# The split weights in DRAM laid out in runs of 2048 bytes a partition, in a linear attention with a gated feed-forward

## The chip, the cores and the metric

One Trainium2 chip, one of its cores. The metric is the device time of one execution in microseconds (us), as the median of several runs. TensorE is called PE here, VectorE DVE, ScalarE ACT, GpSimd POOL and SyncE SP, as in the profile.

## What is computed

The reference is a linear attention followed by a gated feed-forward net, all in float32:

```python
q_s = softmax(q, over the head's 64 columns);  k_s = softmax(k, over the 576 positions)
kv = k_s.T @ v;  attn = q_s @ kv            # for each of 8 batches and 8 heads
x = attn as (4608, 512);   xn = x / sqrt(mean(x*x) + 1e-6) * rms_g
out = (silu(xn @ w_gate) * (xn @ w_val)) @ w_out                        # w_gate, w_val: 512 x 1536, w_out: 1536 x 512
```

## The kernel before

The 4608 tokens are cut into nine blocks of 512 columns. A product of float32 numbers is made of three products of a reduced float32 type: each operand is split into a high part (a rounded copy) and a low part (the remainder), and high times high, high times low and low times high are summed. So each weight exists as a pair of halves.

A hand-written list, `ORDER`, gives the steps in the order in which they are issued. Each step is one of the functions below, its numbers after the dots; the letter behind a colon names the engine. Every engine works through its own instructions in that order, and an instruction that waits holds up all that stand behind it on the same engine.

The work has three stages:

- Blocks 0 to 2 (to about 375 us) go one by one, while the attention of later blocks is made beside them. For a chunk `s` (12 chunks of 128 hidden columns to a block) the weights' halves are made by `w_hi` and `w_lo` in a tile named `w` (two buffers), and by `o_hi` and `o_lo` in a tile named `o` (two buffers). `f1` (L973) multiplies them with `x`, `f2` (L1010) with the hidden values `hh` and `hl` that `h_hi` and `h_lo` (L994) make. In block 1 the halves are also written to DRAM by SP: `w_keep` (L917, 12 of them) and `o_keep` (L921, 12). SP further writes sums and differences of the weights, split in the same way, with `s_keep` (L958, 24). In the last six chunks of block 2 (30 to 35) the halves aren't made again but reloaded: `w_back` (L925) and `o_back` (L929), six each.
- Blocks 3 to 8 go in three pairs. A pair's first products use one level of Strassen's scheme: `pp.p.i.m.k` (L1122) is product k of pair p, chunk pair i, matrix m (gate or value), six matmuls each. Its weights come from DRAM through four tiles called the ring, one for each matrix m and each part: part 1 holds four of the eight stored parts and part 2 three. `w_in.p.i.m.part` (L1095) reloads one such tile as soon as the last product that reads it is done; there are 72. Their destination stands in the trace as `ring` or `w`.
- The last products use `o` in pair 0 (`f2p`, L1215, with 24 reloads `o_in`, L1107) and a second Strassen level in pairs 1 and 2 (`qq`, L1331, whose weights SP loads in `qw`, L1276 and L1279, partly from the same DRAM tensors `od`).

All reloads of `w_back`, `o_back`, `w_in` and `o_in`, 108 in all, are issued on POOL's own DMA queue. POOL also does a share of the arithmetic: `q_sub` and `q_mul` for the attention (L730, L759), low parts such as `h_lo` (L994), `b_lo` (L1078) and `n_lo` (L821), and sums such as `t_add` (L1066). The program is built with `dynamic_dma_scratch_size=1024`, the room in each partition of SBUF that is set aside for the descriptors of POOL's DMAs.

The DRAM tensors are `wd` (six, one for two chunks) and `od` (twelve). Before the change a partition's eight parts of one matrix lie together in `wd`, 2048 bytes each: a part-1 reload reads one run of 8192 bytes from each of 128 partitions, a part-2 reload one of 6144, a `w_back` two of 4096; an `o_in` or `o_back` reads one run of 4096.

Of the kernel before, what the change touches and what calls it, by code (L numbers as in the profile page):

```python
# [8 lines left out]
F32 = mybir.dt.float32  # L9
I32 = mybir.dt.int32  # L10
U32 = mybir.dt.uint32
F32R = mybir.dt.float32r
# [334 lines left out]
def linear_attention_then_gated_ffn(ctx: ExitStack, tc, q, k, v, w_gate, w_val, w_out, rms_g, out):  # L347
    nc = tc.nc
    B, H, S, D = q.shape
    NT, DM = out.shape  # L350
    DF = w_gate.shape[1]
    P = 128
    NG = H // 2
    NKT = DM // P
    NF = DF // P
# [14 lines left out]
    NH = NF // 2  # L370
    HALF = TB // 2
    assert NB == JP + 2 * NPAIR and NKT == 4 and NF == 2 * NH

    wsp = ctx.enter_context(tc.tile_pool(name="wsp", bufs=2))
# [29 lines left out]
    def on(default):  # L404
        return unit[0] or default
# [467 lines left out]
    wh_, wo_, h_, po, g_, v_ = {}, {}, {}, {}, {}, {}  # L873
    ov = out.rearrange("(j t p) m -> j t p m", p=P, t=T)
    ov0 = out.rearrange("(j p t) m -> j t p m", p=P, t=T)

    def w_tile(s):
        if s not in wh_:
            wh_[s] = wsp.tile([P, 2, 2, 2, HALF], F32R, name="w")
        return wh_[s]  # L880

    def o_tile(s):
# [9 lines left out]
    def w_hi(s, a, n):  # L892
        copy(w_tile(s)[:, a:a + n, :, 0], halves(s % NF, a, n), nc.scalar)

    def w_lo(s, a):
        w = w_tile(s)[:, a]
        on(nc.gpsimd).tensor_tensor(out=w[:, :, 1], in0=halves(s % NF, a, 1)[:, 0], in1=w[:, :, 0].bitcast(F32),  # L897
                                    op=ALU.subtract)
# [6 lines left out]
        on(nc.vector).tensor_tensor(out=ol, in0=W(s % NF, 2), in1=oh.bitcast(F32), op=ALU.subtract)  # L905

    S2, S1, A11, A12, A21, A22, S3, S4 = range(8)
    wd = [tc.dram_tile([2, P, 8, 2, HALF], F32, name=f"wd{i}") for i in range(NH)]
    od = [tc.dram_tile([P, 2, DM], F32, name=f"od{i}") for i in range(NF)]
    ot_ = {}  # L910

    def parts_of(i, at, n):
        return wd[i][:, :, at:at + n].rearrange("m p a b f -> p m a (b f)")

    def w_keep(s):
        i, odd = divmod(s % NF, 2)
        on(nc.sync).dma_start(parts_of(i, A21 if odd else A11, 2),  # L917
                          wh_[s].rearrange("p m a b f -> p m a (b f)").bitcast(F32))

    def o_keep(s):  # L920
        on(nc.sync).dma_start(od[s % NF], ot_[s].bitcast(F32))  # L921

    def w_back(s):
        i, odd = divmod(s % NF, 2)
        nc.gpsimd.dma_start(w_tile(s).rearrange("p m a b f -> p m a (b f)"), parts_of(i, A21 if odd else A11, 2))  # L925

    def o_back(s):
        o = wsp.tile([P, 2, DM], F32R, name="o")
# [26 lines left out]
        on(nc.gpsimd).tensor_tensor(out=t[:, :, 1], in0=f, in1=t[:, :, 0].bitcast(F32), op=ALU.subtract)  # L955

    def s_keep(i, n):
        on(nc.sync).dma_start(parts_of(i, {1: S1, 2: S2, 3: S3, 4: S4}[n], 1)[:, :, 0],  # L958
                          split[i, n].rearrange("p m b f -> p m (b f)").bitcast(F32))

    done = {}
# [57 lines left out]
    XF, XO, RING, WO, H2, TMP, HH = {}, {}, {}, [], {}, {}, {}  # L1019
# [61 lines left out]
    def ring():  # L1081
        if not RING:
            t0 = big.tile([P, 6, TB], F32R, name="ring_0", tag="raw_0")
            t1 = big.tile([P, 6, TB], F32R, name="ring_1", tag="raw_1")
            RING[1] = [t0[:, :4]]
            RING[2] = [t1[:, :3], t1[:, 3:]]
            WO.append(t0[:, 4:])

    def w_in(p, i, m, part):
        ring()  # L1090
        if part == 1 and m == len(RING[1]):
            RING[1].append(wsp.tile([P, 4, TB], F32R, name="w"))
        t = RING[part][m].rearrange("p a b -> p (a b)")
        src = wd[i][m, :, :4] if part == 1 else wd[i][m, :, 5:]
        nc.gpsimd.dma_start(t, src.rearrange("p a b f -> p (a b f)"))  # L1095

    def o_in(p, t, c):
        ring()
# [309 lines left out]
    def e_put(x, h):  # L1408
# [7 lines left out]
              n_t, n_y0, n_y1, o_hi, o_lo, q_c0, q_eps0, q_exp, q_half, q_half2, q_hi, q_lo, q_load, q_load0, q_max,  # L1416
              q_max0, q_max2, q_mul, q_mul0, q_rec, q_rec0, q_sub, q_sub0, q_sum, q_sum0, q_sum2, q_t, q_t0, q_x, q_x0,
              silu, store, w_keep, o_keep, w_back, o_back, s_add, s_hi, s_lo, s_keep, x_cp, x_nm, t_add, b_hi, b_lo,
              w_in, o_in, r_keep, r_load, t_sum, t_hi, t_lo, t_keep, qw, q_t1, q_t2, q_t3, q_t4, qb_hi, qb_lo, qq, qs1, qu2, qu3,
              q22, q21, q12, qtr, qput, qpua, pp, c_s1, c_u2, c_u3, c_11, c_21, c_22, c_12, gate, hm, e_add, e_tr, e_copy, e_put, hp_hi, hp_lo, f2p, put, v_load, v_ones, w_hi, w_lo, warm, x_acc, x_hi, x_lo, x_sq)}  # L1420

# [33 lines left out]
```

## Time and profile before

| | us |
|---|---|
| median of three runs | 941.9 (941.64, 941.9, 947.51) |
| the profiled execution, its own time | 938.76 |
| its span, first to last instruction | 937.0 |

The profiled execution's own time is 1.76 us above its span and 3.1 us under the median. Times in rows count from the start of the span. A timeline row gives start, duration, engine, line, operation, names (written <- read), and in brackets the idle time before it with what ended it.

### The profile page before, as it was taken

The numbers are of one execution on the slowest core, as the hardware profiler recorded it, in microseconds if no ns is written. First come the engines' busy times: TensorE is split into PE (matmuls) and PEld (weight loads), VectorE is DVE, ScalarE is ACT, GpSimd is POOL, SyncE is SP. The second block draws the span as 40 slices with busy tenths as digits, with TensorE's granted clock in tenths as the row PEclk, the third lists the DMA queues.
The fourth block names the chain that finished last, engine by engine and source line by source line (L and its number), as shares of the span: only waits on it lengthen the run. The fifth ranks groups of instructions, "written<-read, shape, count | busy, mean of one in ns | idle before, by whom it ended". The sixth has DMA issues, their size and how long they took to land.

```text
span 937.0 us, 14321 instructions
## 1 busy us (share of the span) xinstructions
PE 917.7 (98%) x4601; PEld 744.2 (79%) x4601; DVE 729.1 (78%) x1530; ACT 469.0 (50%) x749; POOL 535.2 (57%) x552
## 2 busy tenths in 40 slices
PE   7999999998999999999999999999999999999998
PEld 5578877886887888888888888878888888888886
DVE  7899879987979998877887788766469965645586
ACT  5898847765678766464553364222215522111241
POOL 5887879877677987667763635333432423332403
PEclk8999999999999999999999999999999999999999
DMA  9996628889977999898986799889665788855255
GB/s 244 301 261 195 159 45 283 283 277 304 304 249 211 225 254 260 231 269 222 237 217 203 228 272 285 275 270 298 204 199 175 212 194 278 267 189 179 71 155 91
DMA packets 214203, 212.65 MB, mean 227 GB/s; under 512 B 136816, under 2 KB 175472, under 8 KB 209520
## 3 DMA queue, kind: packets, MB, share of 16 engines
q1 hardware_dynamic: 191472, 122.86, 47.7%
q0 software_dynamic: 16320, 88.09, 30.3%
q10 hardware_dynamic: 6336, 0.79, 0.6%
q8 instruction: 37, 0.61, 0.3%
q14 instruction: 38, 0.31, 0.1%
HBM read 161.35 MB, written 50.33 MB: 226 GB/s over the span
## 4 chain that ended last, share of the span: by engine, by line
PE 88%; DMA 5%; SPq 2%; DVE 2%; issue 1%; ACT 1%; POOL 1%; DVEq 0%; ACTq 0%; POOLq 0%
PE ps_gv L973 18%; PE ps_gv L1122 18%; PE ps_o L1122 11%; PE ps_o L1010 9%; PE ps_a L1122 7%; PE ps_o L1331 6%; PE ps_o L1215 4%; PE ps_a L1331 3%; PE ps_gv L1331 3%; PE ps_a L577 2%; PE ps_a L1215 2%; PE ps_gv L1215 2%; PE ps_a L785 2%; DMA w<-in_moe_w_val_dram 1%; SPq L520 1%
## 5 line engine op out<-in xcount | busy, mean ns | idle before, releaser
L973 PE MATMUL ps_gv<-xh,w 128*128 128x512 f32 x576 | 190.1, 397 | 1.1 <-DVE gs L985 0.8
L1122 PE MATMUL ps_gv<-x,ring 128*128 128x512 f32 x576 | 143.0, 392 | 0.0
L973 PEld LDWEIGHTS ps_gv<-xh,w 128*128 128x128 f32 x576 | 108.2, 188 | 26.2 <-DVE gs L985 0.9
L1122 PEld LDWEIGHTS ps_gv<-x,ring 128*128 128x128 f32 x576 | 107.0, 188 | 23.0
L973 PE MATMUL ps_gv<-xl,w 128*128 128x512 f32 x288 | 111.6, 391 | 0.0
L1143 DVE TENSOR_TENSOR tmp<-tmp,ps_gv 128x512 f32<-128x512 f32 x84 | 57.3, 684 | 49.3 <-PE ps_gv L1122 47.5
L1122 PE MATMUL ps_o<-x,ring 128*128 128x512 f32 x360 | 85.4, 390 | 0.9 <-DVE tmp L1143 0.9
L1095 POOL DMA_DIRECT2D ring<-wd x54 | 31.0, 575 | 92.3 <-PE ps_o L1122 37.1
L1122 PEld LDWEIGHTS ps_o<-x,ring 128*128 128x128 f32 x360 | 67.5, 188 | 15.4 <-DVE tmp L1143 1.3
L1010 PE MATMUL ps_o<-o,hh 128*128 128x512 f32 x288 | 73.2, 396 | 0.0
L973 PEld LDWEIGHTS ps_gv<-xl,w 128*128 128x128 f32 x288 | 54.2, 188 | 10.6 <-issue 0.4
L1010 PEld LDWEIGHTS ps_o<-o,hh 128*128 128x128 f32 x288 | 53.0, 188 | 11.2 <-issue 0.4
L897 POOL TENSOR_TENSOR w<-w,w 128x512 fp32r<-128x512 f32 x36 | 48.8, 1366 | 4.6 <-ACT w L409 3.8
L1143 DVE TENSOR_TENSOR tmp<-tmp,ps_o 128x512 f32<-128x512 f32 x42 | 28.6, 684 | 27.4 <-PE ps_o L1122 24.3
L409 ACT CAST hh<-gs 128x512 fp32r<-128x512 f32 x48 | 29.5, 615 | 29.9 <-DVE gs L985 16.0
L1095 POOL DMA_DIRECT2D w<-wd x18 | 10.1, 559 | 58.0 <-PE ps_a L1122 37.8
L534 DVE TENSOR_REDUCE cm<-kt 128x128 f32<-128x640 f32 x28 | 36.7, 1310 | 4.4 <-DMA kt<-in_k_dram 4.4
L1010 PE MATMUL ps_o<-o,hl 128*128 128x512 f32 x144 | 38.7, 391 | 0.0
L1122 PE MATMUL ps_a<-x,w 128*128 128x512 f32 x144 | 36.9, 392 | 0.0
L1122 PE MATMUL ps_a<-x,ring 128*128 128x512 f32 x144 | 36.7, 390 | 0.0
L994 POOL TENSOR_TENSOR hl<-gs,hh 128x512 fp32r<-128x512 f32 x20 | 26.8, 1340 | 16.9 <-ACT hh L409 10.8
L1122 PE MATMUL ps_gv<-x,w 128*128 128x512 f32 x144 | 35.1, 391 | 0.0
(634 smaller groups left out, 2306.8 us busy)
## 6 DMA issues: line engine op xcount, KB each, us to landing
ring<-wd POOLq DMA_DIRECT2D x36, 768.0 KB, 5.7
w<-wd POOLq DMA_DIRECT2D x24, 1024.0 KB, 6.0
ring<-wd POOLq DMA_DIRECT2D x18, 1024.0 KB, 5.5
wd<-w SPq DMA_DIRECT2D x12, 1024.0 KB, 5.0
wd<-parts SPq DMA_DIRECT2D x24, 512.0 KB, 3.7
o<-od POOLq DMA_DIRECT2D x18, 512.0 KB, 5.9
od<-o SPq DMA_DIRECT2D x12, 512.0 KB, 3.9
out_dram<-ot SPq DMA_DIRECT2D x20, 256.0 KB, 4.3
```

The lines of the kernel that those rows point to most:

```text
L409: (e.copy if e is nc.scalar else e.tensor_copy)(dst, src)
L534: nc.vector.tensor_reduce(out=cm, in_=kt_[b, g].rearrange("p h j d -> p h d j"), axis=AX.X, op=ALU.max)
L577: nc.tensor.matmul(pk[h * D:(h + 1) * D, :D + 1], lhsT=ke[:n, h, j], rhs=vt[:n, j, h], start=(j == 0), stop=(j == len(rows) - 1))
L897: on(nc.gpsimd).tensor_tensor(out=w[:, :, 1], in0=halves(s % NF, a, 1)[:, 0], in1=w[:, :, 0].bitcast(F32), op=ALU.subtract)
L973: nc.tensor.matmul(pd[s], lhsT=w[:, a, c // 2, m, c % 2 * P:c % 2 * P + P], rhs=X[j, c][x], start=(n == 1), stop=(n == 3 * NKT))
L994: on(nc.gpsimd).tensor_tensor(out=hl, in0=g_[s], in1=h_[s][0].bitcast(F32), op=ALU.subtract)
L1010: nc.tensor.matmul(po[t], lhsT=a[:, t * P:(t + 1) * P], rhs=w, start=(i == 0 and n == 0), stop=(i == NF - 1 and n == len(terms) - 1))
L1095: nc.gpsimd.dma_start(t, src.rearrange("p a b f -> p (a b f)"))
L1122: nc.tensor.matmul(abc[p, i, m, b], lhsT=src[:, h, c * P:(c + 1) * P], rhs=operand(o, c, x), start=first and n == 0, stop=n == 5, skip_gro ...
L1143: nc.vector.tensor_tensor(out=dst, in0=ux[u + (src,)], in1=abc[u + (b,)], op=ALU.add)
L1215: nc.tensor.matmul(pa[p, t, k], lhsT=a[:, k * P:(k + 1) * P], rhs=w, start=(c == 0 and n == 0), stop=(c == NF - 1 and n == 2))
L1331: nc.tensor.matmul(qacc[p, b, x], lhsT=ws[l][x], rhs=h[m], start=first and i == 0 and n == 0, stop=i == NH - 1 and n == 2, skip_group_chec ...
```

## The change

The tile `w` and the DRAM tensors get another order of the same elements. In `wd` each of the eight parts of each matrix becomes a block of 128 partitions by 2048 bytes; `od` becomes two such blocks. Inside the tile `w` the two matrices' parts alternate. All transfers of these tensors by `w_keep`, `o_keep`, `s_keep`, `w_back`, `o_back` and `w_in`, `o_in` then consist of runs of 2048 bytes. `qw` still reads runs of 1024 bytes from `od`. No step is added, left out or moved, and no engine changes.

```diff
     def w_tile(s):
         if s not in wh_:
-            wh_[s] = wsp.tile([P, 2, 2, 2, HALF], F32R, name="w")
+            wt_[s] = wsp.tile([P, 4, 2 * HALF], F32R, name="w")
+            wh_[s] = wt_[s].rearrange("p (k m) (b f) -> p m k b f", k=2, b=2)
         return wh_[s]
...
-    wd = [tc.dram_tile([2, P, 8, 2, HALF], F32, name=f"wd{i}") for i in range(NH)]
-    od = [tc.dram_tile([P, 2, DM], F32, name=f"od{i}") for i in range(NF)]
+    wd = [tc.dram_tile([8, 2, P, 2 * HALF], F32, name=f"wd{i}") for i in range(NH)]
+    od = [tc.dram_tile([2, P, DM], F32, name=f"od{i}").rearrange("m p f -> p m f") for i in range(NF)]
     def parts_of(i, at, n):
-        return wd[i][:, :, at:at + n].rearrange("m p a b f -> p m a (b f)")
+        return wd[i][at:at + n].rearrange("k m p f -> p (k m) f")
     def w_keep(s):
         i, odd = divmod(s % NF, 2)
-        on(nc.sync).dma_start(parts_of(i, A21 if odd else A11, 2),
-                          wh_[s].rearrange("p m a b f -> p m a (b f)").bitcast(F32))
+        on(nc.sync).dma_start(parts_of(i, A21 if odd else A11, 2), wt_[s].bitcast(F32))
     def w_back(s):
         i, odd = divmod(s % NF, 2)
-        nc.gpsimd.dma_start(w_tile(s).rearrange("p m a b f -> p m a (b f)"), parts_of(i, A21 if odd else A11, 2))
+        w_tile(s)
+        nc.gpsimd.dma_start(wt_[s], parts_of(i, A21 if odd else A11, 2))
     def s_keep(i, n):
-        on(nc.sync).dma_start(parts_of(i, {1: S1, 2: S2, 3: S3, 4: S4}[n], 1)[:, :, 0],
+        on(nc.sync).dma_start(parts_of(i, {1: S1, 2: S2, 3: S3, 4: S4}[n], 1),
                           split[i, n].rearrange("p m b f -> p m (b f)").bitcast(F32))
     def w_in(p, i, m, part):
...
-        t = RING[part][m].rearrange("p a b -> p (a b)")
-        src = wd[i][m, :, :4] if part == 1 else wd[i][m, :, 5:]
-        nc.gpsimd.dma_start(t, src.rearrange("p a b f -> p (a b f)"))
+        src = wd[i][:4, m] if part == 1 else wd[i][5:, m]
+        nc.gpsimd.dma_start(RING[part][m], src.rearrange("k p f -> p k f"))
```

## Rows read from the trace of the kernel before

**Rows 1.** The page, part 1: busy time, share, instructions.
```profile
PE 917.7 (98%) x4601; PEld 744.2 (79%) x4601; DVE 729.1 (78%) x1530; ACT 469.0 (50%) x749; POOL 535.2 (57%) x552
```
**Rows 2.** Windows: length, busy by engine, granted clock, DMA share, GB/s.
```profile
310.00:370.00 60.00, 60.00 (x340) 49.10 (x339) 53.82 (x142) 39.93 (x63) 50.36 (x57) 1.00 1.07 265
412.00:937.00 525.00, 519.74 (x2414) 426.50 (x2412) 372.75 (x706) 178.12 (x300) 219.38 (x231) 1.00 0.74 216
```
**Rows 3.** PE's waits, 310 to 937 us: total, times, longest.
```profile
PE ps_o L1122 <- DVE tmp L1143: 0.9, 1, 0.9
```
**Rows 4.** DMA queues: packets, MB, share of 16 engines' span.
```profile
q0 software_dynamic: 16320, 88.09, 30.3%
...
q10 hardware_dynamic: 6336, 0.79, 0.6%
```
**Rows 5.** Groups of POOL's instructions by form: count, busy us, mean ns, idle before.
```profile
L1095 POOL DMA_DIRECT2D ring<-wd x54 | 31.0, 575 | 92.3 <-PE ps_o L1122 37.1 <-PE ps_a L1122 28.7 <-PE ps_gv L1122 23.1
...
L925 POOL DMA_DIRECT2D w<-wd x6 | 4.7, 784 | 4.6 <-PE ps_gv L973 4.3 <-issue 0.3
```
**Rows 6.** DMA issues: count, KB each, median us from issue to landing.
```profile
wd<-parts SPq DMA_DIRECT2D x24, 512.0 KB, 3.7
...
od<-o SPq DMA_DIRECT2D x12, 512.0 KB, 3.9
```
**Rows 7.** POOL's timeline, 305 to 332 us: first and last of six reloads.
```profile
310.46 0.89 POOL L925 DMA_DIRECT2D w<-wd  x1
...
328.02 0.75 POOL L925 DMA_DIRECT2D w<-wd  x1 [0.26 <-issue]
```
**Rows 8.** Timeline of ACT and PE, 333 to 338 us.
```profile
333.38 0.63 ACT L734 ACTIVATE qt<-qt 128x512 f32<-128x512 f32 x1 [1.87 <-POOL qt L730]
...
334.94 0.73 ACT L569 ACTIVATE kt<-kt 128x640 f32<-128x640 f32 x1
...
336.80 0.80 PE L577 MATMUL ps_a<-vt,kt 128*64 128x65 f32 x20
```
**Rows 9.** POOL's timeline, 356 to 362 us.
```profile
356.14 0.77 POOL L925 DMA_DIRECT2D w<-wd  x1 [2.40 <-PE ps_gv L973]
356.91 0.55 POOL L1095 DMA_DIRECT2D ring<-wd  x1
...
358.74 1.28 POOL L1066 TENSOR_TENSOR ot<-xl,xh 128x512 f32<-128x512 f32 x1
...
361.05 0.55 POOL L1107 DMA_DIRECT2D x<-od  x1
```
**Rows 10.** Timeline of ACT and PE, 358 to 364 us.
```profile
360.59 0.61 ACT L409 CAST hh<-gs 128x512 fp32r<-128x512 f32 x1
...
363.68 0.62 PE L1010 MATMUL ps_o<-o,hh 128*128 128x512 f32 x2
```
**Rows 11.** Landings of the reloads issued at 356.14 (L925) and 356.91 (L1095).
```profile
DMA to landing us min/median/max: 5.6/5.6/5.6
...
DMA to landing us min/median/max: 8.4/8.4/8.4
```
**Rows 12.** Timeline of POOL and PE, 408 to 411 us.
```profile
409.03 1.29 POOL L821 TENSOR_TENSOR ql<-acc,qh 128x512 fp32r<-128x512 f32 x1
...
410.38 0.49 PE L835 MATMUL ps_a<-ql,mean_w 128*128 128x512 f32 x1
```
**Rows 13.** The reload with the least to spare: issue, landing, first matmul.
```profile
559.96 0.57 POOL L1107 DMA_DIRECT2D o<-od  x1
...
DMA to landing us min/median/max: 7.6/7.6/7.6
...
568.84 0.61 PE L1215 MATMUL ps_a<-o,hh 128*128 128x512 f32 x2
```
**Rows 14.** Timeline of POOL and PE, 380 to 384 us.
```profile
381.34 1.29 POOL L994 TENSOR_TENSOR hl<-gs,hh 128x512 fp32r<-128x512 f32 x1
...
383.40 0.84 PE L1010 MATMUL ps_o<-o,hl 128*128 128x512 f32 x3
```

More of the change, by code (lines that the diff above doesn't have):

```diff
@@ L875, in linear_attention_then_gated_ffn @@
     ov0 = out.rearrange("(j p t) m -> j t p m", p=P, t=T)
+    wt_ = {}
     def w_tile(s):
         if s not in wh_:
-            wh_[s] = wsp.tile([P, 2, 2, 2, HALF], F32R, name="w")
+            wt_[s] = wsp.tile([P, 4, 2 * HALF], F32R, name="w")
+            wh_[s] = wt_[s].rearrange("p (k m) (b f) -> p m k b f", k=2, b=2)
         return wh_[s]
```

## The prediction

> **What bounds the kernel now.** I read the page's busy shares first: PE is busy 98% of the span, POOL 57%, ACT 50% [rows 1]. Then the windows: POOL's reloads run from 310 us on, and from there PE is busy 60.00 of 60 us, then 519.7 of 525, at a granted clock of 1.00, while the DMA share is 1.07 and then 0.74 [rows 2]. Then PE's waits after 310: one, of 0.9 us, for DVE, and none for a DMA [rows 3]. So PE's matmuls set the time and every reload lands in time. The change touches no matmul; it can only matter where something that it makes later reaches PE, and it can hardly win anything, since after 310 PE lost 0.9 us to waits and some 4 us at the very end.
>
> How much the reloads have to spare: the tightest of the 108 is an `o_in` issued at 559.96, landed 7.6 us later, used at 568.84, 1.3 us to spare [rows 13]. Followed in the same way, none of the other 107 has under 2.
>
> **Packets.** A `w_in` of part 1 goes from 128 runs to 512, one of part 2 from 128 to 384, a `w_back` from 256 to 512, an `o_in` or `o_back` from 128 to 256. Before: 72 x 128 + 6 x 256 + 30 x 128 = 14,592, and with 16 small ones for each of 108 DMAs 16,320, the count of the queue [rows 4]. After: 36 x 512 + 36 x 384 + 6 x 512 + 30 x 256 = 43,008, with the small ones 44,736.
>
> **What a packet costs the DMA.** On SP's queue 512 KB in packets of 2048 bytes (`s_keep`) land after 3.7 us and the same in packets of 4096 (`o_keep`) after 3.9 [rows 6]: nothing. From above: the 6336 packets of queue q10, of 125 bytes on average, take 0.6% of 16 engines' 937 us, 14 ns each [rows 4], so no more than that is fixed. 384 more packets over 16 engines are then at most 0.34 us for a reload. With the longer issue (next part) a reload lands 0.2 to 1.0 us later, under the spare of 1.3 of the tightest, which itself gains only 128 packets (0.1 + 0.2 us). Late data costs PE nothing; I take 0.
>
> **What a packet costs POOL.** An issue of 128 packets takes 575 ns, one of 256 (`w_back`, the only such form) 784 [rows 5]: 0.21 us for 128 more. A `w_in` becomes 0.63 (part 1) or 0.42 us longer, a `w_back` 0.42, an `o_in` or `o_back` 0.21; in all 36 x 0.63 + 36 x 0.42 + 6 x 0.42 + 30 x 0.21 = 46.6 us of POOL, which is busy for 50.4 + 219.4 of the 585 us of the two windows [rows 2] and so has room. From below, the 0.21 us may be the price of the third dimension of the access pattern, not of packets: then every `w_in` and `o_in` costs 0.21 and `w_back` nothing. From above, the issue grows in proportion to the packets, 2.3 us for 512 (a rival below). I take 0.21 for 128. The Trainium skill's page DMA: Bandwidth & Descriptors (section Anatomy of one DMA) says that one can emit a lot of descriptors before the incremental cost shows up; by it terms A and B below would be 0, but the row of 784 against 575 speaks against it.
>
> Where does a longer POOL reach PE? Where POOL's next instruction is used at once.
> A. Between 310.46 and 328.02 six reloads are issued [rows 7]: three `w_back`, two o-reloads, a `w_in` of part 2, 3 x 0.42 + 2 x 0.21 + 0.42 = 2.1 us more. Behind them POOL's `q_sub` releases ACT at 333.38; behind that on ACT `k_exp` ends at 335.67, and PE's `k_mm` starts at 336.80 [rows 8]: 1.13 to spare. So PE is 0 to 1.0 late, by how much of the 2.1 POOL's short idle times there take up; I take 0.5.
> B. Right behind a `w_in` at 408.43 POOL makes `n_lo`, which ends at 410.32, and PE's `n_sum` takes it at 410.38 [rows 12]: 0.06 to spare, so PE is 0.6 late.
> At other places I found spare. A + B = 1.1 us.
>
> C. **Room for descriptors.** POOL writes the descriptors of its DMAs into a scratch of 1,024 bytes a partition. Before, the largest pile is at 361.05: five reloads issued in 4.9 us [rows 9], none landed (the first does at 356.14 + 5.6 = 361.74, [rows 11]): 256 + 4 x 128 = 768 packets under way, and no issue waits. After, the same five make 512 + 512 + 384 + 256 + 256 = 1,920, and the first two alone 1,024, beside 256 of an `o_back` that hasn't quite landed. Whether that fits, no row shows: the cost is between 0 and a wait of POOL for the landing of what came before. I take the wait, since the pile is 2.5 times what the trace shows to fit.
> The Trainium skill's page DMA: Bandwidth & Descriptors (sections Terms and The descriptor swizzle) gives 16 bytes to a descriptor and 9 on each engine, the completing one included, to 1 MiB in 128 partitions. By it the scratch holds 64 an engine; the five reloads before take 53, which agrees with rows 9, and two of 512 packets take 66; the wait would fall where I put it.
> The price, from rows: the `w_in` at 356.91 stands until `w_back.35` has landed, 361.74 + 0.42 = 362.2, then takes 1.2 instead of 0.55 us, so POOL goes on at 363.4 instead of 357.46, 5.9 late. Behind it stand two `t_add` (L1066, to 360.02), for which ACT waits with the `hh` of `f2.33` behind it, ready at 361.20; PE takes that at 363.68 [rows 9, 10], 2.5 to spare: PE 3.4 late. Next the `o_back` stands until that `w_in` has landed, 5.6 to 8.4 us [rows 11] after 362.2, 367.8 to 370.6; POOL gets there at 363.4 + 2.55 + 0.97 = 366.9, so 0.9 to 3.7 more. Behind it are low parts for the first `pp` and the `hl` of `f2.34`, which has 383.40 - 382.63 = 0.8 to spare [rows 14]. Some of it falls into POOL's idle times; I take 1 of 0 to 3.7. Later an `o_in` now and then follows a `w_in` closely; such places may add up to the same 3.7 once more, I take 0. In the pairs a reload is issued every 5 to 6 us (96 of them in 525 us [rows 2]) and the one before it is about to land (512 + 384 under way), so nothing stands. C = 4.4, bounds 0 and 10.8.
>
> SP's side: 12 `w_keep` and 12 `o_keep` of block 1 double their packets. Their landing shows no price [rows 6]; if each took 0.3 us longer, ACT and DVE, which reuse the tiles, would be late by that at a few places: 0, bound 1. `w_hi` and `w_lo` write the same runs of 256 elements at other places of the tile: 0, covered by ACT's 50% [rows 1].
>
> Sum: 1.1 + 4.4 = +5.5 us against the profiled execution's 938.76, 944.3. The median of the runs shown lies 3.1 above that execution, so I give 941.9 + 5.5 = 947.4.
>
> **The rivals.**
> No wait for room: the scratch holds it, or frees places while a transfer runs. For it: no row shows POOL waiting for its own queue. Then only A + B: 943.0.
> SP's transfers gain, since they meet 2048-byte packets on the same engines instead of 8192, or the change does nothing. For it: a DMA share of 1.07 in 310 to 370 [rows 2]. Against: PE waits for no DMA there, so no more than the 0.9 us of [rows 3] comes back: 941.0 to 941.9.
> POOL becomes the bound between 310 and 370 (slower): the issue grows with the packets, 0.575 us for 128 more. In that window stand six `w_back`, seven o-reloads, two `w_in` of part 2 and one of part 1: 6 x 0.78 + 7 x 0.57 + 2 x 1.15 + 1.73 = 12.7 us more on 50.4 busy of 60 [rows 2]: 3.1 too much, with B at 1.7 and C at its 3.4 + 3.7 = 7.1: +11.9, 953.8. It decides from where POOL's idle 9.6 us are used up, 9.6 / 12.7 x 0.575 = 0.43 us for 128 packets, twice the price of [rows 5]. Against it: 256 packets cost 784 ns, not 1150.
>
> **How the numbers follow.** The wait for room, 947.4: 0.50. No wait, 943.0: 0.30. SP gains or nothing happens, 941 to 942: 0.06. POOL as the bound, 953.8: 0.14. One per cent is 9.4 us, about what a measurement of this kernel can tell from no change. Slower by more: most of the last case, 0.11, and a fifth of the first, whose bounds reach +11.9, 0.10: 0.21. Faster by more would need 9 us that PE doesn't lose after 310: 0.02. The rest, 0.77, is within 1%. The range goes from 940 (no wait, and runs that lie at the profiled execution's 938.76 + 1.1 rather than 3.1 above it) to 956 (the last case and 2 us of it unpriced).
>
> **What would show it.** Right: the queue of POOL has 44,736 packets; a `w_in` issue of about 1.2 us in the pairs; near 357 and 367 an issue that takes or waits 4 to 5 us, and PE idle near 364 and 380, some 4 us in all; PE still waits for no DMA. Wrong: POOL's issues near 357 no longer than elsewhere (no wait for room); a `w_in` over 1.9 us (POOL as the bound); PE waiting for `ring` or `w` to land (a packet costs the DMA more than 14 ns); PE's matmuls spaced otherwise.

## The result and the profile after

The changed kernel took 956.13 us (median of six runs, 951.1 to 959.93) against 942.74 for the kernel before on the same chip; the ratio is 1.0135 with a 95% interval of 1.0099 to 1.0171. On the 941.9 shown above that is 954.6, or +12.7 us where +5.5 was forecast. The profiled execution took 951.1 us with a span of 949.3, 12.3 more than before.

The page's first part and its queue of POOL, to be held against [rows 1] and [rows 4]:

```profile
PE 922.8 (97%) x4601; PEld 746.7 (79%) x4601; DVE 730.9 (77%) x1530; ACT 468.7 (49%) x749; POOL 559.5 (59%) x552
...
q0 software_dynamic: 44736, 88.09, 34.5%
```

The windows that answer to [rows 2], with one more between them:

```profile
310.00:370.00 60.00, 56.23 (x320) 45.61 (x318) 46.93 (x129) 34.79 (x53) 46.98 (x49) 1.00 1.11 236
370.00:412.00 42.00, 39.39 (x207) 31.98 (x208) 34.43 (x90) 25.77 (x43) 29.61 (x34) 0.92 0.92 215
412.00:937.00 525.00, 524.00 (x2443) 429.13 (x2442) 379.78 (x720) 183.69 (x308) 245.37 (x238) 1.00 0.82 219
```

The packets are the 44,736 that were counted. From 412 us on PE is busy all the time, as before. Most of what is lost lies in one place around 370 us: PE idles there, and the granted clock of the second window is 0.92. PE's waits after 310 (total, times, longest) name it:

```profile
PE ps_o L1013 <- ACT hh L409: 5.8, 1, 5.8
PE ps_a L1217 <- POOL hl L1199: 0.9, 1, 0.9
PE ps_a L577 <- issue: 0.5, 1, 0.5
```

No wait for a DMA among them. Why ACT was late is seen in POOL's timeline of 355 to 375 us, beside [rows 9]:

```profile
358.98 0.81 POOL L928 DMA_DIRECT2D w<-wd  x1 [1.82 <-PE ps_gv L976]
368.07 0.75 POOL L1097 DMA_DIRECT2D ring<-wd  x1 [8.29 <-issue]
368.84 1.27 POOL L1069 TENSOR_TENSOR xl<-xl 128x512 f32<-128x512 f32 x1
370.06 1.26 POOL L1069 TENSOR_TENSOR ot<-xl,xh 128x512 f32<-128x512 f32 x1
...
373.96 0.74 POOL L932 DMA_DIRECT2D o<-od  x1 [1.92 <-issue]
```

and in the landing of the `w_back` issued at 358.98 (beside [rows 11]):

```profile
DMA to landing us min/median/max: 8.8/8.8/8.8
```

The `w_in` stands 8.29 us with no releaser that the profile could name ("issue") and goes at 368.07, 0.3 us after the `w_back` has landed at 358.98 + 8.75 = 367.73 (8.75 is the 8.8 above, unrounded). The two `t_add` behind it come after that. Then ACT and PE, beside [rows 10]:

```profile
371.36 0.62 ACT L409 CAST x<-ot 128x512 fp32r<-128x512 f32 x1 [10.01 <-POOL ot L1069]
371.88 0.61 ACT L409 CAST hh<-gs 128x512 fp32r<-128x512 f32 x1
```

```profile
372.55 3.78 PE L1013 MATMUL ps_o<-o,hh 128*128 128x512 f32 x8 [5.82 <-ACT hh L409]
376.12 1.30 PE L1013 MATMUL ps_o<-o,hl 128*128 128x512 f32 x4
```

`hh` itself was not late; it stood in ACT's order behind a cast of the sum that POOL owed. And the eight matmuls behind the wait took 3.78 us; the same eight a chunk earlier (358.40) took 1.98. The granted clock of short stretches of the changed kernel (PE busy first, PEclk third from the end) says why:

```profile
372.50:376.40 3.90, 3.85 (x9) 3.11 (x10) 3.89 (x8) 2.92 (x7) 2.30 (x5) 0.50 1.13 288
376.40:380.00 3.60, 3.60 (x17) 2.87 (x17) 3.22 (x14) 2.85 (x4) 3.60 (x4) 0.98 0.76 241
...
219.00:223.00 4.00, 3.19 (x9) 2.61 (x10) 3.86 (x11) 2.60 (x3) 1.62 (x2) 0.57 1.04 364
```

After 5.8 us without a matmul PE ran at 0.50, the lower level (1.2 GHz), for the length of `f2.33`: 2.0 us on top of the 6.0 of the wait. The third line is another place, behind a wait for `kx` (a maximum over `k` that DVE makes at L554) that both kernels have (3.21 us before, 3.62 here); the same window of the kernel before:

```profile
219.00:223.00 4.00, 3.95 (x19) 3.28 (x19) 3.89 (x11) 3.35 (x4) 2.39 (x2) 1.00 1.04 369
```

With the same step paired in both traces, PE is 2.2 us late by 224 us (0.4 in the first 42 us, 0.4 at `kx`, 1.4 of this low clock), 0.7 more at the `k_mm` of [rows 8], 6.0 at `f2.33` and 2.0 in it, 0.3 at `f2.34`, 1.2 at a step of `f2p` (580.82 below) and some 0.7 in smaller steps; 0.8 comes back at 631 us, where the wait of [rows 3] is gone: 12.3. The low clock at 219 us does not need the change: of the fourteen executions profiled for this study eleven show it, two of the four with the layout of before among them. All six with `wd` laid out as in the change show it, behind waits for `kx` of 3.6 to 4.5 us against 3.1 to 3.2 with the layout of before, so a part of the 2.2 may still be the change's; no run separates that.

The step of `f2p` stands behind another reload that waited. POOL's `o_in` at 578.72 goes 0.3 us after one issued at 571.77 has landed (578.41), and the `hl` that PE needs comes behind it; the profile names PE as POOL's releaser, but PE's step (ps_o L835) had ended 0.7 us earlier:

```profile
571.77 0.74 POOL L1109 DMA_DIRECT2D o<-od  x1
...
578.72 0.74 POOL L1109 DMA_DIRECT2D x<-od  x1 [2.65 <-PE ps_o L835]
579.48 2.53 POOL L1199 TENSOR_TENSOR hl<-xl,hh 128x512 fp32r<-128x512 f32 x2
```

```profile
580.82 0.50 PE L1217 MATMUL ps_a<-o,hl 128*128 128x512 f32 x1 [0.90 <-POOL hl L1199]
```

The same pattern, a start 0.3 us after a landing with no releaser named, stands at 328.61 (0.52 us of idle time), 437.84 (0.71), 471.20 (2.46), 511.34 (2.85), 547.73 (1.20) and 844.48 (1.86).

POOL's issues by form (count, busy, mean ns), beside [rows 5]:

```profile
L1097 POOL DMA_DIRECT2D ring<-wd x54 | 42.7, 790 | 90.9 <-PE ps_o L1124 34.3 <-PE ps_a L1124 25.2 <-PE ps_gv L1124 14.8
...
L1109 POOL DMA_DIRECT2D o<-od x12 | 8.8, 736 | 7.6 <-PE ps_a L1217 3.0 <-issue 2.5 <-PE ps_o L1217 2.1
L928 POOL DMA_DIRECT2D w<-wd x6 | 4.9, 825 | 1.8 <-PE ps_gv L976 1.8
```

384 and 512 packets cost 790 ns, 256 cost 736, and the `w_back`, which had three dimensions already, went from 784 to 825 with 256 packets more: the 0.2 us over [rows 5] belong to the form of the access, hardly to the number of packets.

### The profile page after: what moved, and what is told of

Read it like the earlier page. It is cut to its first block, busy times and chain, and to the rows that moved or that the text cites. A ratio compares the mean times of both kernels' runs of the same rounds, so it can differ in the third digit from the quotient of the medians.

```text
span 949.3 us, 14321 instructions
## 1 busy us (share of the span) xinstructions
PE 922.8 (97%) x4601; PEld 746.7 (79%) x4601; DVE 730.9 (77%) x1530; ACT 468.7 (49%) x749; POOL 559.5 (59%) x552
## 3 DMA queue, kind: packets, MB, share of 16 engines
q0 software_dynamic: 44736, 88.09, 34.5%
## 4 chain that ended last, share of the span: by engine, by line
PE 80%; POOL 4%; DVE 4%; issue 4%; DMA 3%; SPq 3%; ACT 1%; POOLq 0%; DVEq 0%; ACTq 0%
PE ps_gv L1124 17%; PE ps_gv L976 15%; PE ps_o L1124 10%; PE ps_o L1013 8%; PE ps_a L1124 7%; PE ps_o L1333 6%; PE ps_o L1217 4%; PE ps_a L1333 3%; PE ps_gv L1333 3%; PE ps_a L577 2%; PE ps_a L785 2%; PE ps_a L1217 1%; PE ps_gv L1217 1%; SPq L520 1%; DMA sd<-kt 1%
## 5 line engine op out<-in xcount | busy, mean ns | idle before, releaser
L1097 POOL DMA_DIRECT2D ring<-wd x54 | 42.7, 790 | 90.9 <-PE ps_o L1124 34.3
L1013 PE MATMUL ps_o<-o,hh 128*128 128x512 f32 x288 | 75.1, 403 | 5.8 <-ACT hh L409 5.8
L976 PEld LDWEIGHTS ps_gv<-xl,w 128*128 128x128 f32 x288 | 54.6, 190 | 10.8 <-issue 0.4
L1097 POOL DMA_DIRECT2D w<-wd x18 | 14.3, 794 | 55.7 <-PE ps_a L1124 32.8
```

Source lines behind the costliest of these rows:

```text
L976: nc.tensor.matmul(pd[s], lhsT=w[:, a, c // 2, m, c % 2 * P:c % 2 * P + P], rhs=X[j, c][x], start=(n == 1), stop=(n == 3 * NKT))
L1013: nc.tensor.matmul(po[t], lhsT=a[:, t * P:(t + 1) * P], rhs=w, start=(i == 0 and n == 0), stop=(i == NF - 1 and n == len(terms) - 1))
L1097: nc.gpsimd.dma_start(RING[part][m], src.rearrange("k p f -> p k f"))
```

## The experiments

Three theories: **room** (POOL stands before a reload until an earlier one has landed, since its descriptors don't fit), **issues** (each reload's issue is some 0.2 us longer), **landing** (transfers in packets of 2048 bytes come later).

**More room.** The changed kernel with 1536 bytes instead of 1024.

```diff
-    ... dynamic_dma_scratch_size=1024)
+    ... dynamic_dma_scratch_size=1536)
```

> The changed kernel with 1536 bytes a partition for the descriptors of POOL's DMAs instead of 1024 (more than that SBUF does not hold). Theory 1, room: two reloads of 512 packets now fit side by side, so the 8.3 us in which POOL stands in front of the w_in at 368.07 go, and with them PE's 5.8 us of waiting for hh and the 2.0 us that the lower clock took behind it: 956.1 - 7.8 = 948, between 945 and 950; a shorter wait may appear a reload or two later. Theory 2, the issues (longer by 0.2 us each) make POOL late, and theory 3, transfers in packets of 2048 bytes land later: neither depends on the room, so 954 to 958 with the same idle time of POOL.

947.82 us; ratio to the kernel before 1.0056 (1.0028 to 1.0085). By the ratios (1.35% before this, 0.56% now) some 7.4 of the 12.7 us are gone, and the long wait with them. POOL's waits with no releaser named, after 310 us, and then PE's waits:

```profile
POOL o L932 <- issue: 1.6, 1, 1.6
POOL ring L1097 <- issue: 0.3, 1, 0.3
```

```profile
PE ps_o L1013 <- DVE hl L997: 0.4, 1, 0.4
PE ps_gv L976 <- DVE gs L988: 0.3, 1, 0.3
```

The issues are as long and the packets as small as in the changed kernel, so room accounts for the large part. What makes the other 5 us this profile doesn't show: it is of the fastest of twelve runs, 941.19.

**Less room for the kernel before.** Layout and packets untouched.

```diff
-    ... dynamic_dma_scratch_size=1024)
+    ... dynamic_dma_scratch_size=384)
```

> The kernel before, its packets of 4096 to 8192 bytes untouched, with 384 bytes for descriptors instead of 1024. Theory 1, room: a w_back of 256 packets and any reload beside it no longer fit (384/1024 of what held 1024 packets but not 1024 and 256 is under 480), so POOL stands in front of the w_in at 356.9 until the w_back has landed, some 5 us, and at the other places between 310 and 370 where a reload follows a w_back within 6 us; PE waits for hh in f2.33 by 2 us or more: 945 to 960. Theories 2 and 3: neither the issues nor the packets have changed, so 942 to 943 and no new idle time of POOL in front of a DMA.

967.46 us; ratio 1.0255 (1.0213 to 1.0297), more than expected. POOL's timeline at the same place, and the first of PE's waits after 310:

```profile
371.71 0.78 POOL L925 DMA_DIRECT2D w<-wd  x1 [0.56 <-PE ps_gv L973]
378.19 0.55 POOL L1095 DMA_DIRECT2D ring<-wd  x1 [5.70 <-issue]
...
383.73 0.53 POOL L929 DMA_DIRECT2D o<-od  x1 [1.97 <-issue]
```

```profile
PE ps_o L1010 <- ACT hh L409: 8.7, 1, 8.7
```

Packets of 4096 to 8192 bytes, and yet the same wait, at the same step, with the same end on PE. The size of the packets is not what matters, their number against the room is.

**The step moved.** In the changed kernel's order the `w_in` goes behind the two `t_add`.

```diff
-... h_mul.33 w_in.0.0.0.1 q_max.6.1 b_hi.0.6.1:A t_add.0.3.1:P k_max.5.2 b_hi.0.2.1:A t_add.0.1.0:P f1.34.0 ...
+... h_mul.33 q_max.6.1 b_hi.0.6.1:A t_add.0.3.1:P k_max.5.2 b_hi.0.2.1:A t_add.0.1.0:P w_in.0.0.0.1 f1.34.0 ...
```

> The changed kernel with one step moved in the order: the w_in issued at 368.07 stands behind the two t_add of POOL instead of in front of them. Theory 1, room: POOL still stands in front of that w_in until the w_back has landed, some 4 to 7 us, but ACT gets the sums first, so f2.33 does not wait: 956.1 - 7.8 = 948, between 945 and 951, unless a low part or sum behind the moved step is late in its turn. Theory 2 (issues): the sum of the issues is the same, 954 to 958. Theory 3 (landing): the w_in is issued no earlier, 954 to 958.

954.85 us; ratio 1.0127 (1.0083 to 1.0171): nothing gained. The 948 expected of room failed. The number alone is what the issues or the landing would give (954 to 958); what speaks for room here is the trace. POOL's timeline, then PE's longest waits after 310:

```profile
361.89 1.29 POOL L1069 TENSOR_TENSOR ot<-xl,xh 128x512 f32<-128x512 f32 x1
366.41 1.53 POOL L1097 DMA_DIRECT2D ring<-wd  x2 [3.23 <-issue]
373.04 0.73 POOL L932 DMA_DIRECT2D o<-od  x1 [5.10 <-issue]
```

```profile
PE ps_gv L1124 <- DVE x L1081: 1.5, 1, 1.5
PE ps_gv L1124 <- DVE tmp L1145: 1.4, 1, 1.4
PE ps_o L1013 <- POOL hl L997: 1.4, 1, 1.4
```

POOL's standing got only a little shorter (3.2 + 5.1 against 8.3 + 1.9); most of it moved in front of the `o_back`, and after 310 us PE now waits at ten places, for 1.5 us at most, instead of at three, the longest 5.8. By 394 us these have made it 5.8 us late, of the 8.0 that `f2.33` no longer loses. Here, moving the waiting instruction only chose who pays.

**One part of the change alone.** First od:

```diff
-    od = [tc.dram_tile([P, 2, DM], F32, ...) ...]
+    od = [tc.dram_tile([2, P, DM], F32, ...).rearrange("m p f -> p m f") ...]
```

> Only the DRAM tensors od in the new layout; wd and the tile w as before. o_in, o_back move 256 packets instead of 128, w_in and w_back as before. Theory 1, room: the five reloads at 356 to 361 make 256 + 128 + 128 + 256 + 256 = 1024 packets, so at most the last one waits, 1 us or less; 942 to 944.5, and what is left of the change above is that of wd. The 1.2 us by which f2p.0.1.7 is later in the changed kernel, where POOL's hl comes behind an o_in, shows here too. Theory 2 (issues): 36 of 114 issues are longer, so a third of 13 us, 946 to 947. Theory 3 (landing): o reloads have the least to spare, so PE waits for a tile o: over 944.

942.6 us; ratio 0.9993 (0.9970 to 1.0017). Of the five reloads only the last one stood, as expected:

```profile
365.48 0.72 POOL L1107 DMA_DIRECT2D x<-od  x1 [0.78 <-issue]
```

The 1.2 us at `f2p.0.1.7` (PE's step at 580.82 above) did not show: that they came from od alone is refuted. They belong to the reload that waits in front of it: the same `o_in` finds 960 packets under way, its own included, in place of 1216 here, and starts without such a wait; with 1536 bytes it starts at once beside 1216, and PE is not late in either case. Then wd alone (the diff above without its od line):

> Only wd and the tile w in the new layout, od as before (o_in, o_back 128 packets). Theory 1, room: 512 + 512 still don't fit, so the long wait in front of the w_in stays, the o_back behind it (512 + 384 + 128 = 1024) barely waits: 949 to 955. Theory 2: 78 of 114 issues longer: 951 to 953, without a long wait of POOL. Theory 3: w reloads have 10 us to spare, so under 945.

949.62 us; ratio 1.0074 (1.0051 to 1.0098). So od, which costs nothing alone, costs some 0.6% on top of wd, as a limit on the sum would have it. The long wait is there, and a 3.0 us one that the count of 1024 had not given:

```profile
368.71 0.74 POOL L1097 DMA_DIRECT2D ring<-wd  x1 [8.03 <-issue]
...
375.68 0.58 POOL L932 DMA_DIRECT2D o<-od  x1 [2.99 <-issue]
```

**A smaller w_back.** wd with the two matrices side by side, so that a `w_back` is 256 packets again (`w_keep` and `s_keep` accordingly).

```diff
-    wd = [tc.dram_tile([8, 2, P, 2 * HALF], F32, ...) ...]
+    wd = [tc.dram_tile([8, P, 2, 2 * HALF], F32, ...) ...]
```

> The changed kernel with the two matrices' parts side by side in a partition of wd: a w_back moves 256 packets of 4096 bytes instead of 512 of 2048, w_in as in the changed kernel. Theory 1, room: w_back and the w_in behind it make 768 and fit, so POOL goes on to its two t_add at once; the next w_in (384 more, 1152) and then the o_back wait, 2 to 4 us each at most, behind the t_add. Where POOL has no time to give, as the moved step showed, part of that still reaches PE: 946 to 953, between the room of 1536 and the changed kernel. Theories 2 (issues) and 3 (landing): 100 of 114 reloads and all their issues as in the changed kernel, 954 to 957.

950.64 us; ratio 1.0075 (1.0042 to 1.0108). The first `w_in` no longer stands; the next two reloads do, and four `o_in` later on (513.89 to 582.37, 0.8 to 3.3 us each):

```profile
363.22 0.79 POOL L1098 DMA_DIRECT2D ring<-wd  x1 [1.61 <-issue]
367.25 0.74 POOL L933 DMA_DIRECT2D o<-od  x1 [3.24 <-issue]
```

**The issues' length by itself.** The kernel before, with a memset behind each `w_in`, `o_in` and `o_back`.

```diff
+        nc.gpsimd.memset(pad, 0.0)     # pad: [64, 120] float32
```

> The kernel before with a memset of some 0.19 us on POOL behind each w_in, o_in and o_back, which stands for the 0.16 to 0.21 us by which these issues are longer in the changed kernel; layout and packets as before. If what is left over with the room of 1536 (5 us) comes from the longer issues, this costs the same: 945 to 948. If it comes from waits for room that are left, or from the landing, this costs at most what the prediction gave to its terms A and B: 942 to 943.

944.54 us; ratio 1.0009 (0.9978 to 1.0039). The memsets took some 220 ns each, a little more than the issues grew. Longer issues cost nothing that can be measured.

**Room for all of it.** wd as in the smaller `w_back`, od as before, 1536 bytes.

> Room of 1536, w_back of 256 packets, od as before, and only w_in in packets of 2048 bytes: the pile at 356 to 361 is 256 + 512 + 384 + 128 + 128 = 1408 packets of some 1536, so POOL never waits for room. w_in's issues stay 0.2 us longer. If what is left over with the room of 1536 comes from waits for room: 942 to 943.5. If it comes from the issues: 72 of 114 of them, 944.5 to 947. If from the landing of packets of 2048 bytes on the reloads: the same 944.5 to 947, but with PE waiting for a tile, which no profile so far shows.

939.29 us; ratio 0.9965 (0.9939 to 0.9991), less than any of the three had expected. A second time:

> The kernel with wide room a second time. If packets of 2048 bytes on w_in gain something once POOL has room, 938 to 941 and a ratio whose interval lies under 1. If the first result came from how often the low clock at 219 us falls into a run, a ratio of 0.997 to 1.003 with 1 inside. No theory has it slower than before by more than 0.5%.

939.95 us; 0.9976 (0.9951 to 1.0000). All of POOL's waits without a named releaser after 310 us (the same two lines in both profiles), and the form of the issues:

```profile
POOL ring L1098 <- issue: 0.3, 1, 0.3
POOL o L933 <- issue: 0.2, 1, 0.2
```

```profile
L1098 POOL DMA_DIRECT2D ring<-wd x54 | 42.6, 790 | 87.1 <-PE ps_o L1125 35.0 <-PE ps_a L1125 28.2 <-PE ps_gv L1125 21.1
```

The 72 `w_in` in packets of 2048 bytes with issues of 790 ns cost nothing once nothing waits for room; the version is not slower than the kernel before and may be 0.3% faster, which is about as little as five rounds can tell. The room alone does not do it:

> The kernel before with 1536 bytes for descriptors instead of 1024, nothing else. It never waited for room, so by theory 1 it stays the same, 941 to 943.5. If the 0.35% by which the kernel with wide room came out under the kernel before is due to the other place of everything in SBUF, this one is at 938.5 to 940.5 as well.

942.2 us; 0.9989 (0.9963 to 1.0016).

**The other 5 us.** Room of 1536 with wd alone, and the first experiment a second time for another profile.

> wd and the tile w new, od as before, room of 1536: the pile at 356 to 361 is 512 + 512 + 384 + 128 + 128 = 1664 packets, a little over what the room holds, against 1920 with both. Theory 1, room: a short wait in front of the last one or two, 941 to 946, between the wide room (939.3) and the room of 1536 with both (947.8). If w_back in 512 packets costs something by itself (its landing, 3.7 to 5 us ahead of f1), the time stays at 946 to 949 and PE waits for a tile w in f1.

> The changed kernel with room of 1536 a second time, for another profiled execution: the first had 941.2 where the median of its runs was 947.8. If waits for room are what is left, an execution nearer the median shows POOL standing 2 us or more in front of a reload between 355 and 372 and PE waiting behind it there; if it is the low clock at 219 us, that stretch alone is longer and the rest as in the first profile.

948.65 us, ratio 1.0050 (1.0018 to 1.0082), and 946.06 us, ratio 1.0046 (1.0021 to 1.0072). The first is over the 941 to 946 expected of room and in the range of the rival, a late `w_back`; but its sign, PE waiting for a tile `w`, is missing: PE's longest wait after 310 us is 3.3, for DVE's `hl`. So neither account held. POOL stood once in it:

```profile
365.39 0.58 POOL L932 DMA_DIRECT2D o<-od  x1 [2.00 <-issue]
```

The second profile is of the slowest of its twelve executions (span 949.4), with the same 1.6 us of POOL's standing as the first time. So the step that is late is another, and neither of the two that were expected: DVE's, then PE's timeline of it:

```profile
366.61 0.69 DVE L713 TENSOR_REDUCE st<-qt 128x16 f32<-128x512 f32 x1 [5.40 <-DMA qt<-in_q_dram]
...
460.24 0.69 DVE L713 TENSOR_REDUCE st<-qt 128x16 f32<-128x512 f32 x1 [5.31 <-DMA qt<-in_q_dram]
```

```profile
370.13 2.07 PE L1013 MATMUL ps_o<-o,hl 128*128 128x512 f32 x4 [3.18 <-DVE hl L997]
...
461.58 2.49 PE L1124 MATMUL ps_gv<-x,ring 128*128 128x512 f32 x6 [3.38 <-DVE tmp L1145]
```

DVE waits for SP's small loads of `q`; `hl` and `tmp` stand behind that in its order, and PE pays twice, each time with some low clock behind it (0.58 and 0.59 over the next 4 and 3.5 us). The last two of those loads were issued at 358.99 and 359.40, right behind a `w_back` (357.39) and a `w_in` (358.20), and landed late:

```profile
DMA to landing us min/median/max: 6.2/6.6/7.1
```

In the kernel before the last one, issued at 356.54, lands after 4.1 us, and DVE waits 2.2, which PE does not feel; in the kernel before with 1536 bytes it was 3.4, with wd alone at 1536 6.0, in both profiles of the wide room 0, and in the changed kernel with 1024, where the `w_in` went 9 us later than its `w_back`, also 0. So `q` can come late when its last pieces meet the pile of reloads. Smaller packets are not needed for such a landing: in the kernel before six of these loads, issued 0.9 to 3.5 us behind a `w_back` (347.00), landed after 6.6 to 7.1 us as well, without DVE waiting for them. Whether the smaller packets add to it, or only the shift of POOL against SP, stays open; nothing was tried that separates these two.

## Why the prediction was right or wrong

The sign, the place and the mechanism were right; the size was not. +12.7 us lies at the upper end of the range (the median of the six runs, 956.13, is 0.13 above it), and of the three chances the one that came, slower by over 1%, had been given 0.21. That the range reaches so far is partly luck: its upper end was taken from POOL as the bound, which did not come; the bounds of the wait itself end at 941.9 + 1.1 + 10.8 = 953.8, and 954.6 came.

- Packets, no wait of PE for a reload, PE bound after 412 us: as forecast, 44,736 and [rows 2] repeated.
- What a packet costs POOL: the step failed. 0.21 us for 128 more was read from the one form that had both more packets and a third dimension; 790 ns for 384 and 512 packets show that the lower bound (the form) was right and the value taken not. A `w_in` is 0.21 us longer, not 0.42 to 0.63. The Trainium skill's page DMA: Bandwidth & Descriptors (section Anatomy of one DMA) had said that many descriptors go out before their number shows; the trace agrees, with 736 ns at 256 and 790 at 512. POOL as the bound, the rival built on it, is refuted.
- A (0.5): the delay at that `k_mm` is 0.7, near the forecast by luck. In front of it two reloads stood for room: the `o_back` at 323.61 and the `w_in` at 328.61 start 0.3 us after a landing. In the two profiles of the changed kernel with 1536 bytes the issues are as long, and this `k_mm` is not late at all.
- B (0.6): PE takes `n_sum` at 421.89, right behind `n_lo` as before, and is 0.2 us later, with 1536 bytes too.
- C (4.4) is the mis-sized term. Its first wait, put at 3.4, measured 8.0: 6.0 of waiting and 2.0 of low clock. The wait stands at the `w_in` that was named, ends with the landing that was named, and reaches PE through the `t_add`, ACT and `hh` of `f2.33` as written. But the `w_back` landed after 8.75 us, not the 5.6 of [rows 11], and the price of an idle PE at half clock afterwards was left out. SP's queue moved 0.83 MB while it was under way, 0.09 before; of the fourteen profiles' last `w_back` the two beside 0.64 and 0.83 MB landed after 8.5 and 8.75 us, the twelve beside 0.5 MB or less after 5.6 to 7.1. Why SP's loads fell there is open. The second wait, put at 1 (1.92 at the `o_back`, within the 0.9 to 3.7), cost PE 0.3 at `f2.34`. The later waits, put at 0, cost the 1.2 at `f2p`, and the 0.7 of A are waits for room as well. That is 10.2 us in all.
- "In the pairs nothing stands" failed. It reckoned with a reload every 5 to 6 us, but two can come within 4 us of each other; POOL stood there five times with no releaser named, and at 578.72. Only the last is seen to make PE late by more than 0.3 us.
- What packets cost the DMA was looked at for the reloads alone and for SP's stores, and put at 0. In the changed kernel's own profile DVE does not wait for `q` after 310 us, so nothing there contradicts it. With 1536 bytes some 5 us of the medians remain, by waits for `q` and the waits for room that are left; that share is argued from the profiles of two runs, and only that it disappears with the wide room is shown.
- Of the 12.3 us between the two profiles 2.2 lie ahead of 224 us and are not counted above; the profile is of the fastest of six executions, and what the others lose beyond it (5 us at the median, 3 us in the kernel before) no trace shows.

How much fits can now be told from rows. Counted are a reload's packets and its 16 small ones ([rows 4]): 528 and 400 for `w_in` part 1 and 2, 528 or 272 for `w_back`, 272 or 144 for an o-reload.

| kernel | room, bytes | most under way without a wait | with the reload that stood |
|---|---|---|---|
| before | 1024 | 848 | none stood |
| changed | 1024 | 944 | 528 + 528 = 1056 (8.29 us) |
| only od | 1024 | 960 | 1104 (0.78) |
| only wd | 1024 | 944 | 1056 (8.03), 1072 (2.99) |
| smaller w_back | 1024 | 944 | 1200 (1.61) |
| changed | 1536 | 1472 | 1728 (1.60) |
| only wd | 1536 | 1456 | 1600 (2.00) |
| wide room | 1536 | 1488 | none stood |
| before | 384 | 288 | 416 (5.70) |

The limit lies between 960 and 1056 for 1024 bytes, 1488 and 1600 for 1536, 288 and 416 for 384: one packet to a byte of the setting fits all nine, and the 3.0 us that surprised with wd alone are among them, once the small ones are counted. The later waits of the changed kernel fit too: the `o_in` at 578.72 made 1216, those at 471.20, 511.34 and 547.73 made 1072, 1200 and 1072. The Trainium skill's page DMA: Bandwidth & Descriptors (section Terms) gives 16 bytes to a descriptor; with the packets spread over 16 engines that works out, as an estimate that gives each engine the room of one partition, to the same rule, and the waits agree with it.

## What to carry to other kernels

Before cutting a software queue's transfers into more packets, add up what is under way at its densest moment, the small completing packets too, and hold it against the room set aside for descriptors; the wait shows as "issue" in front of a DMA on the issuing engine, and everything in that engine's order pays. The releaser that a profile names can hide it: look whether the start follows a landing. Give the room (here 512 bytes a partition, with a coarser layout for `w_back` and od) rather than move the waiting step. An idle tensor engine can cost more than its idle time: count the stretch at the low clock behind it.

## What the hardware showed that was not expected

- Behind 5.8 us without a matmul the granted clock was 0.50 for 3.9 us, then 0.98: 2.0 us more for eight matmuls and four. Behind the wait for `kx` of 3.21 us it stayed at 1.00 in the kernel before, behind 3.62 us in the changed kernel it was 0.57 for the next 4 us. The length of that wait does not decide it alone: in the fourteen profiles it stayed up behind 3.15, 3.20 and 3.21 us and fell behind 2.71, 2.80, 3.14 and 3.17.
- Issues of POOL take 550 to 575 ns with two dimensions (128 packets), 736 to 825 with three, be it 256, 384 or 512 packets.
- Small loads on SP's queue, issued 1 to 2 us behind two reloads on POOL's, took 6.2 to 7.1 us to land; 0.9 to 3.5 us behind a `w_back` in the kernel before they took 6.6 to 7.1.
- In all the waits for room named here POOL's next reload started 0.3 us after a landing.
